# A new order of single operations within a chunk's period, and a skip term added in PSUM

## The chip, the cores and the metric

One Trainium2 chip, one core. The metric is the device time of one execution in microseconds (us). The kernel is written in Bass with the Tile framework. Its engines are TensorE (PE, with its weight loads as PEld), VectorE (DVE), ScalarE (ACT), GpSimd (POOL) and SyncE (SP, which here only issues DMAs). POOL issues DMAs too, into a queue of its own ("software dynamic" in the profile; SP's is "hardware dynamic").

## The reference

Two layers, each an S4 state-space convolution and a SwiGLU feed-forward block, on one sequence of L = 2048 positions with D = 512 channels (N = 128 states per channel, F = 1376). Cut to what matters:

```
def A(u, A_re, A_im, B, C, log_dt, Dskip):      # u is layernorm(x)
    dt = exp(log_dt)
    P  = exp(dt * (A_re + i*A_im) * l)          # l = 0 .. L-1
    K  = sum over n of (C * P * dt * B).real    # [D, L]: one filter per channel
    y  = causal convolution of u with K, along the sequence (by FFT)
    return y + u * Dskip
def B(x): return (silu(x @ w_gate) * (x @ w_up)) @ w_down
x = x + A(layernorm(x)); x = x + B(layernorm(x))   # twice, with the same weights
```

The skip term u * Dskip is a convolution with a filter that is Dskip at lag 0. So the kernel adds Dskip to the filter's value at lag 0 and has no other code for it. That one addition is "skip" below.

## The kernel before, in words

The program has two parts. The first, the **kernel stage** (until about 245 us of the span), computes the filters K and their spectra. The second takes the spectra through the convolutions and the two feed-forward blocks; a short **passage** (some 245 to 335 us), in which the weights are scaled and the first blocks are convolved, joins them. In the second part a scheduler sets the order, and the order of its instructions is the same in both kernels.

In the kernel stage the 512 channels are cut into NCH = 8 chunks of DC = 64 channels. The filter is split by lag into two factors: P over l is a product of a coarse factor (64 values, tiles `re` and `im`, in the big tile `wall`; buffer c % 2 for chunk c) and a fine one (32 values, tile `g`, two buffers). What is done for each chunk:

- `gen_turns`: phases, by integer additions on DVE (`xz` and the upper half of `im`; in the listing TENSOR_TENSOR wall<-tdk, then four ISA wall<-wall, each twice as long as the last).
- `gen_trig`, `gen_exp`: sines, cosines, exponentials on ACT, with a change of ACT's function table (ACT_TABLE_LOAD) between them.
- `gen_e`: four products on DVE that make `re` and `im` of the coarse factor.
- `gen_g`: the fine factor by doubling, n = 1, 2, 4, 8, 16. Each level is a product with the real part (L491), a product with the imaginary part into a scratch tile (L502), and an addition (L505). For n = 16 and chunks 1 to 6 the second product (L494) goes into the other, free half of the next chunk's `g` buffer, and the addition is done by a DMA with accumulation, issued by POOL (L495, g<-g, 1 MB). So this DMA stands in for a DVE addition.
- `lags`: 128 matmuls on PE (L515, L516) contract the two factors over the states: pk[32, 64] for each channel. They read all of `g`, and `re` and `im` of the chunk.
- `spread_in`: ACT copies pk out of PSUM to `ks` (L526).
- `spread`: SP writes `ks` to DRAM (`kdr`, L533) and reads it back in four DMAs, one per 32 partitions (L535), into `kt`, which has the lags on partitions. For the last two chunks `spread_pe` does it instead with 16 matmuls by pieces of the identity (L542) into `kp`, and an ACT copy to `kt` (L544).
- `skip`: adds Dskip to partition 0 of `kt` (L522). Partition 0 comes with the first of the four reads. It runs on DVE for chunks 0 to 6 and on POOL for chunk 7.
- `spectra` (for chunk 7 `first_parts` and `later_parts`): matmuls of `kt` with DFT constants (L550, L595), copies by ACT, stores to DRAM (`wo`, `spare`, `wa`). `sizes` sums |kt|.

Mixed into this are the norms of the feed-forward weights (`weights`: POOL loads pieces `st`, three buffers; ACT squares them, L353; PE sums them, L356; DVE takes the maximum, L359) and the spectra of the second input block (`second_block`).

Engines run their own instructions in order and wait for each other by semaphores. In the kernel stage no scheduler sets that order: it is written by hand, as a **plan**. A period of 28 to 31 units has one chunk in each state: `use(i)` for chunk i, `factors(i + 1)`, `prepare(i + 2)`. Each step is put into the plan at a number, `at(t + 7.1, copy)`, the plan is sorted by these numbers, and the steps are then issued one after the other. A generator is cut by `yield` into the pieces that can have a number of their own. The numbers give the order of issue only. No engine waits for one of them.

A DVE instruction that reads what an earlier DVE instruction wrote waits for a semaphore that the earlier one raises at its end.

```
            V.tensor_tensor(g[:, :, n:2 * n], g[:, :, 0:n], zr.to_broadcast([P, 2, n, DC]), OP.mult)
            if n == 16 and 0 < ch < NCH - 1:
                tmp = gs[ch + 1][:, :, 16:32]
                V.tensor_tensor(tmp, g[:, ::-1, 0:16], ...)
                G.dma_start(g[:, :, 16:32]..., tmp..., accum_op=OP.add)
```

Of the kernel before, what the change touches and what calls it, by code (L numbers as in the profile page):

```python
# [32 lines left out]
DC = 64  # L33
# [44 lines left out]
def kernel(ctx, tc, x, a_re, a_im, b_re, b_im, c_re, c_im, log_dt, d_skip,  # L78
# [114 lines left out]
    dsk, th32 = tdk[0:1, 0], tdk[:, 1]  # L193
    nc.sync.dma_start(dsk, d_skip)
# [263 lines left out]
    def gen_e(ts):  # L458


        re, im, mu = ts[:3]
        half = [[t.rearrange("p a (g h d) -> p a g h d", g=4, h=2)[:, :, :, o] for t in (re, mu)] for o in range(2)]
        V.tensor_tensor(im[:, :32], im[:, 64:32:-1], re[:, :32], OP.mult)
        yield
        V.tensor_tensor(re[:, :32], re[:, 64:32:-1], re[:, :32], OP.mult)
        yield
        V.scalar_tensor_tensor(im[:, 33:64], im[:, 31:0:-1], -1.0, mu[:, 1:], OP.mult, OP.mult)
        yield
        for r, u in half:
            V.tensor_tensor(r[:, 33:64], r[:, 31:0:-1], u[:, 1:], OP.mult)  # L470
            yield

    def gen_g(ch, ts, g):
# [11 lines left out]
        V.tensor_tensor(g[:, 1, 0], g[:, 1, 0], tmp[:, 1, 0], OP.add)  # L485
        for n in (1, 2, 4, 8, 16):
            yield
# [4 lines left out]
            if n == 16 and 0 < ch < NCH - 1:  # L492
                tmp = gs[ch + 1][:, :, 16:32]
                V.tensor_tensor(tmp, g[:, ::-1, 0:16], xz[:, 2:0:-1, lv:lv + 1].to_broadcast([P, 2, 16, DC]), OP.mult)  # L494
                G.dma_start(g[:, :, 16:32].rearrange("p i b d -> p i (b d)"), tmp.rearrange("p i b d -> p i (b d)"),  # L495
                            accum_op=OP.add)
                continue
            step = min(n, 8)
            for b0 in range(0, n, step):
                tmp = tmp8[:, :, :step]  # L500
                o = slice(n + b0, n + b0 + step)
                V.tensor_tensor(tmp, g[:, :, b0:b0 + step], zi.to_broadcast([P, 2, step, DC]), OP.mult)  # L502
                if b0 + step == n:
                    yield
                V.tensor_tensor(g[:, :, o], g[:, :, o], tmp[:, ::-1], OP.add)  # L505
        yield
# [473 lines left out]
    with tc.manual_schedule(engines={mybir.EngineType.Activation, mybir.EngineType.DVE, mybir.EngineType.PE, mybir.EngineType.Pool}):  # L980
# [30 lines left out]
        stats_x = stats(x1, 4, 1.0, then=lambda: (take(gg, 1), take(ge, 1)))  # L1011
# [4 lines left out]
        for g in (gg, gg, ge, gg, gg, gg, gg, gg, gg):  # L1016
# [12 lines left out]
        for g in (gg, ge, gg, ge, ge):  # L1029
# [14 lines left out]
        def prepare(c, t):  # L1044
# [7 lines left out]
            at(t + 0.35, steps["turns"])  # L1052
            at(t + 0.45, tr)
            at(t + 13.0, steps["turns"], 3)
            at(t + 13.2, steps["turns"], 3)
            at(t + 17.0, tr)
            at(t + 8.3, steps["exp"], 100)

        def factors(c, t):
# [7 lines left out]
            if c + 1 < NCH:  # L1067
                at(t + 8.05, lambda: tiles(c + 1))
# [3 lines left out]
            at(t + 0.3, ge)  # L1072
            for k in range(5):
                at(t + 8.2 + k, gg)
            for k in range(4):
                at(t + 22.0 + 0.6 * k, ge, 1 if k < 3 else 100)

        def use(c, t):
# [12 lines left out]
            at(t + 25.0, lambda: sizes(c, kt, box["ks"]))  # L1091
            for q0, ats in list(enumerate(((t + 17.5, t + 25.2, n + 2.1, n + 7.5),
                                      (n + 6.9, n + 14.0, n + 17.3, n + 21.0))))[:2 if c < NCH - 2 else 1]:
                sp = later(lambda q0=q0: spectra(c, kt, q0))
                if c == NCH - 2:
                    tail["sp"] = sp
                    ats = ats[:2]
                for t0 in ats:
                    at(t0, sp)

        def second_block(k, t):
            box = []
            at(t - 3.0, lambda: box.append(second(*sec[k])))
# [24 lines left out]
        for i in range(NCH - 1):  # L1128
# [6 lines left out]
            for k, t0, t1, t2, t3 in ((0, -13.0, 0.25, 13.9, 22.3), (1, 0.3, 14.5, 17.45, 22.9),  # L1135
                                      (2, 15.0, 26.5, 28.05, 36.0)):
                n = ((3, 3, 0), (3, 3, 0), (3, 3, 0), (3, 2, 0), (3, 2, 0), (3, 3, 0), (3, 3, 3))[i][k]
                if i == NCH - 2 and k == 2:
                    t0, t1, t2, t3 = 15.0, 20.0, 24.0, None
# [61 lines left out]
        spread_pe(ks, kts[1])  # L1201
        skip(c, kts[1], G)
# [109 lines left out]
```

## Time and profile before

| | |
|---|---|
| median of 3 runs | 1077.5 us (1077.13 to 1078.07) |
| the profiled execution | 1077.3 us, its span 1075.0 us |
| PE busy, of the span | 1015.1 us (94%), mean granted clock 0.985 |
| DVE busy | 966.5 us (90%) |
| ACT, POOL busy | 544.4 us (51%), 103.9 us (10%) |
| DMA | 139.74 MB, mean 130 GB/s |

The profile tells of one execution. Each row of the timeline has a start and a duration in us, the engine, the line of the code (L494), the operation and its tiles. In brackets stands how long the engine was idle before it and what ended that wait. Matmuls overlap in PE, so that PE's busy time is no measure of how near it is to its limit. For DMAs the profile has the issue (on SP or POOL) and the time from there to the landing.

### The profile page before, as it was taken

To read this page: it belongs to the slowest core of one execution; us is meant where nothing else is said; L and a number is where in the kernel's file an instruction comes from. 1 tells how busy PE (TensorE), PEld (TensorE's weight loads), DVE (VectorE), ACT (ScalarE), POOL (GpSimd) and SP (SyncE) were. 2 spreads that over 40 slices of the span, in tenths; PEclk is the share of its full clock that TensorE was granted. 3 is DMA by queue.
4 is the path that set the end of the run, shared out by engine and by line. 5 is a ranking of instruction groups with operands and counts; after the bars stand their busy time and mean duration, and the time that the engine had idled before them with its cause. 6 is when DMAs were issued, how large, how long until landed. Compare 5 with 4: busy or idle time off the path is not lost.

```text
span 1075.0 us, 22004 instructions
## 1 busy us (share of the span) xinstructions
PE 1015.1 (94%) x8918; PEld 801.8 (75%) x8918; DVE 966.5 (90%) x1405; ACT 544.4 (51%) x1093; POOL 103.9 (10%) x163
## 2 busy tenths in 40 slices
PE   1979999998789999999999999999999999999998
PEld 0868888887677787777868677786868677696774
DVE  8999999999999999999999999999999999983221
ACT  6979888853268264366652235523525442144210
POOL 1112222210000001011000001101000000000000
PEclk9989999998899999999999999999999999999999
DMA  5266777878665444323054463442444244413000
GB/s 215 100 177 180 171 165 182 188 187 270 218 207 160 122 130 151 128 94 70 16 138 140 126 212 112 124 133 100 123 120 121 86 122 139 126 36 64 1 26 20
DMA packets 120104, 139.74 MB, mean 130 GB/s; under 512 B 50609, under 2 KB 75697, under 8 KB 119234
## 3 DMA queue, kind: packets, MB, share of 16 engines
q1 hardware_dynamic: 108098, 112.83, 34.9%
q0 software_dynamic: 11904, 25.50, 10.2%
q8 instruction: 70, 1.15, 0.5%
q14 instruction: 32, 0.26, 0.1%
HBM read 91.36 MB, written 30.67 MB: 114 GB/s over the span
## 4 chain that ended last, share of the span: by engine, by line
DVE 37%; PE 27%; issue 4%; DMA 3%; ACT 3%; POOL 1%; DVEq 0%; SPq 0%; ACTq 0%; POOLq 0%
DVE t L817 5%; PE pgu L938 5%; PE pgu L935 5%; PE pgu L936 5%; DVE yk L820 5%; DVE yk L817 4%; PE py L951 3%; PE py L952 3%; PE py L953 3%; DVE sg L942 2%; DVE yl L236 2%; DVE hl L944 2%; DMA st<-in_B_w_down_dram 1%; PE pi L789 1%; PE pw L550 1%
## 5 line engine op out<-in xcount | busy, mean ns | idle before, releaser
L935 PE MATMUL pgu<-mix,wall 128*128 128x256 f16 x1280 | 299.0, 273 | 5.8 <-DVE sy L629 2.1
L936 PE MATMUL pgu<-mix,wall 128*128 128x256 f16 x1280 | 298.9, 273 | 0.0
L938 PE MATMUL pgu<-mix,wall 128*128 128x256 f16 x1280 | 195.7, 273 | 0.0
L936 PEld LDWEIGHTS <-wall 128*128 128x128 f16 x1280 | 125.2, 98 | 22.6 <-issue 7.0
L935 PEld LDWEIGHTS <-wall 128*128 128x128 f16 x1280 | 125.2, 98 | 16.4 <-issue 0.9
L938 PEld LDWEIGHTS <-wall 128*128 128x128 f16 x1280 | 125.2, 98 | 14.6
L951 PE MATMUL py<-wall,hh 128*128 128x512 f16 (+1 forms) x352 | 133.4, 379 | 0.0
L952 PE MATMUL py<-wall,hh 128*128 128x512 f16 (+1 forms) x352 | 133.4, 379 | 0.0
L953 PE MATMUL py<-wall,hl 128*128 128x512 f16 (+1 forms) x352 | 132.2, 379 | 0.0
L820 DVE TENSOR_TENSOR yk<-yk,t 128x1024 f32<-128x1024 f32 x96 | 117.5, 1224 | 0.5
L817 DVE TENSOR_TENSOR t<-uu,w 128x1024 f32<-128x1024 f32 x96 | 117.5, 1224 | 0.2
L943 ACT ACTIVATE hh<-sg 128x512 f16<-128x512 f32 x80 | 50.2, 627 | 117.4 <-DVE sg L942 117.3
L942 DVE SCALAR_TENSOR_TENSOR sg<-pgu,sc,sg 128x512 f32<-128x512 f32 x80 | 60.0, 750 | 39.2 <-ACT sg L941 39.2
L550 PE MATMUL pw<-kt,ek 128*128 128x256 f32 (+1 forms) x384 | 93.4, 381 | 0.0
L941 ACT ACTIVATE sg<-pgu,sc 128x512 f32<-128x512 f32 x80 | 54.3, 678 | 75.1 <-PE pgu L938 62.1
L550 PEld LDWEIGHTS pw<-kt,ek 128*128 128x128 f32 x384 | 75.0, 199 | 8.4
L944 DVE TENSOR_TENSOR hl<-sg,hh 128x512 f16<-128x512 f32 x80 | 55.3, 691 | 8.7 <-ACT hh L943 8.6
L953 PEld LDWEIGHTS <-hl 128*128 128x128 f16 (+1 forms) x352 | 34.3, 98 | 38.0
L952 PEld LDWEIGHTS <-hh 128*128 128x128 f16 (+1 forms) x352 | 34.4, 98 | 37.7
L951 PEld LDWEIGHTS <-hh 128*128 128x128 f16 (+1 forms) x352 | 34.4, 98 | 37.3
L515 PE MATMUL pk<-wall,g 128*32 128x64 f32 x1024 | 57.4, 288 | 4.9 <-DMA g<-g 3.7
L516 PE MATMUL pk<-wall,g 128*32 128x64 f32 x1024 | 57.8, 287 | 0.7 <-issue 0.7
(276 smaller groups left out, 1930.6 us busy)
## 6 DMA issues: line engine op xcount, KB each, us to landing
uu<-udr SPq DMA_DIRECT2D x96, 256.0 KB, 3.0
w<-wdr SPq DMA_DIRECT2D x96, 256.0 KB, 2.7
g<-g POOLq DMA_DIRECT2D x6, 1024.0 KB, 9.1
udr<-fu POOLq DMA_DIRECT2D x22, 256.0 KB, 3.2
udr<-u SPq DMA_DIRECT2D x16, 256.0 KB, 3.3
kdr<-ks SPq DMA_DIRECT2D x6, 512.0 KB, 3.1
kt<-kdr SPq DMA_DIRECT2D x24, 128.0 KB, 3.0
out_dram<-xg SPq DMA_DIRECT2D x12, 256.0 KB, 2.3
```

The source lines that it names most:

```text
L516: PE.matmul(o, lhsT=g[:, 1, :, d], rhs=im[:, 0:64, d], start=False, stop=True, tile_position=(0, 32 * grp))
L550: PE.matmul(pw[:, i], lhsT=e, rhs=kt[:, :, c + 4 * k0:4 * k1:4, :].rearrange("p g k d -> p k g d"), start=c == 0, stop=c == 3)
L817: V.tensor_tensor(t, uu.unsqueeze(2).to_broadcast([P, NQ, 2, 2, DC]), w.unsqueeze(3).to_broadcast([P, NQ, 2, 2, DC]), OP.mult)
L820: V.tensor_tensor(yk, yk, t, OP.add)
L935: PE.matmul(o, lhsT=wgu(wi, k, 0)[:, fs], rhs=nh[:, k], start=k == 0, stop=False)
L936: PE.matmul(o, lhsT=wgu(wi, k, 1)[:, fs], rhs=nh[:, k], start=False, stop=False)
L938: PE.matmul(o, lhsT=wgu(wi, k, 0)[:, fs], rhs=nlo[:, k], start=False, stop=k == 3)
L942: V.scalar_tensor_tensor(sg, pgu[:, 1], sc6[:, 4:5], sg, OP.mult, OP.mult)
L944: V.tensor_tensor(hl[:, f0:f0 + 2], sg, hh[:, f0:f0 + 2], OP.subtract)
L951: PE.matmul(py[r], lhsT=hh[:n, f, rc], rhs=wd(f, 0)[:n], start=f == 0, stop=False)
L952: PE.matmul(py[r], lhsT=hh[:n, f, rc], rhs=wd(f, 1)[:n], start=False, stop=False)
L953: PE.matmul(py[r], lhsT=hl[:n, f, rc], rhs=wd(f, 0)[:n], start=False, stop=f == FT - 1)
```

## The change

Four things are done.

1. **Single operations in the plan.** `gen_g`, `gen_e` and `gen_turns` are cut at more places, and each piece gets a number of its own. The operations on DVE (and some on ACT, PE, POOL and SP) stand in another order. The steps and their sizes stay.
2. **The skip term of the last two chunks** is added by PE: `spread_pe` has one further matmul of 128x16 into 32 partitions for each of four groups, which adds the identity's first 32 columns times `tdk`, the row of Dskip, to `kp` in PSUM. For this the other 127 rows of `tdk` are set to zero (a MEMSET on POOL at the start). The additions on DVE (chunk 6) and POOL (chunk 7) go.
3. **Squares and norms.** ACT's squares of one group of weights in each period stand directly behind `ks`, and the matmuls that sum the other group directly behind `lags`.
4. **BN_STATS and BN_AGGR** of several rows are issued in a staggered way (statistics of the next row ahead of the aggregation of this one).

```diff
+    G.memset(tdk[:, 0], 0.0)
     nc.sync.dma_start(dsk, d_skip)
...
-        for r in range(rows):
-            V.bn_stats(st[:, r], src[:, r])
-            V.bn_aggr(mv[:, r], st[:, r])
+        for r in range(rows + 1):
+            if r < rows:
+                V.bn_stats(st[:, r], src[:, r])
+            if r:
+                V.bn_aggr(mv[:, r - 1], st[:, r - 1])
...
         for n in (1, 2, 4, 8, 16):
-            yield
             V.tensor_tensor(g[:, :, n:2 * n], g[:, :, 0:n], zr.to_broadcast([P, 2, n, DC]), OP.mult)
             if n == 16 and 0 < ch < NCH - 1:
+                yield
                 tmp = gs[ch + 1][:, :, 16:32]
...
                             accum_op=OP.add)
+                yield
                 continue
...
                 V.tensor_tensor(tmp, g[:, :, b0:b0 + step], zi.to_broadcast([P, 2, step, DC]), OP.mult)
-                if b0 + step == n:
-                    yield
+                yield
                 V.tensor_tensor(g[:, :, o], g[:, :, o], tmp[:, ::-1], OP.add)
...
-    def spread_pe(ks, kt):
+    def spread_pe(ch, ks, kt):
...
                 PE.matmul(kp[32 * ga:32 * ga + 32, grp], lhsT=ident[:, 32 * grp:32 * grp + 32], rhs=ks[:, ga],
-                          start=True, stop=True, tile_position=(0, 32 * ga))
+                          start=True, stop=ga > 0, tile_position=(0, 32 * ga))
+                if ga == 0:
+                    PE.matmul(kp[:32, grp, 0], lhsT=ident[:, :32], rhs=tdk[:, 0, ch * DC + 16 * grp:ch * DC + 16 * (grp + 1)],
+                              start=False, stop=True, tile_position=(0, 0))
...
-            for k in range(4):
-                at(t + 0.2 + 2 * k, gg, 2)
+                    [0.2, 0.25, 0.339, 2.3, 2.4, 2.5, 7.316, 9.189, 13.02, 13.06, 13.131, 13.171, 13.231]:
+                at(t + d, gg)
...
-            at(t + 7.1, copy)
+            at(t + 5.104, copy)
             if c == NCH - 2:
-                at(t + 10.0, lambda: spread_pe(box["ks"], kt))
-            at(t + 13.1, lambda: skip(c, kt, V))
+                at(t + 10.0, lambda: spread_pe(c, box["ks"], kt))
+            else:
+                at(t + 13.17, lambda: skip(c, kt, V))
...
-        spread_pe(ks, kts[1])
-        skip(c, kts[1], G)
+        spread_pe(c, ks, kts[1])
```

What stands where is told by the listing of each engine's instructions. The names in it: `kt` is the filter with lags on partitions, `tdk` holds Dskip and phases, `g` the fine factor, `spare` the scratch tile, `xz` small powers, `wall` the coarse factor, `mu` squares of `re`, `cmx` maxima of weights.

DVE, the second half of a chunk's period, before (L505 of level 4 to the last of `gen_e`'s products):

```order
L505 TENSOR_TENSOR g<-g,spare 128x2x256
L491 TENSOR_TENSOR g<-g,xz 128x2x512
L502 TENSOR_TENSOR spare<-g,xz 128x1024
L505 TENSOR_TENSOR g<-g,spare 128x2x512
L491 TENSOR_TENSOR g<-g,xz 128x2x1024
L494 TENSOR_TENSOR g<-g,xz 128x2x1024
L412 TENSOR_TENSOR wall<-tdk,am 128x128
L416 ISA wall<-wall 128x256
L416 ISA wall<-wall 128x512
L522 TENSOR_TENSOR kt_425<-kt_425,tdk 1x4x16
L416 ISA wall<-wall 128x1024
L416 ISA wall<-wall 128x2048
```

The same stretch of DVE in the changed kernel (its lines are numbered 3 to 8 higher here: L512 is the addition, L495 and L510 the two products of a level, L499 the product for the DMA, L415 and L419 the phases, L529 the skip):

```order
L415 TENSOR_TENSOR wall<-tdk,am 128x128
L512 TENSOR_TENSOR g<-g,spare 128x2x256
L419 ISA wall<-wall 128x256
L495 TENSOR_TENSOR g<-g,xz 128x2x512
L510 TENSOR_TENSOR spare<-g,xz 128x1024
L419 ISA wall<-wall 128x512
L419 ISA wall<-wall 128x1024
L512 TENSOR_TENSOR g<-g,spare 128x2x512
L419 ISA wall<-wall 128x2048
L529 TENSOR_TENSOR kt_426<-kt_426,tdk 1x4x16
L495 TENSOR_TENSOR g<-g,xz 128x2x1024
L499 TENSOR_TENSOR g<-g,xz 128x2x1024
```

The phases and the skip have moved from behind the two products of the last level to ahead of them, in between the doubling's steps. Behind L499 there now come the products of `gen_e` at once.

POOL, one period before, from the DMA with accumulation on:

```order
L495 DMA g<-g 128x2x1024
L418 MEMSET wall 128x64
L347 DMA st<-in_B_w_gate_dram 128x344 x3
L553 DMA wdr<-wa 128x3x128 x2
L347 DMA st<-in_B_w_gate_dram 128x344 x2
L441 MEMSET wall 128x64
```

and in the changed kernel (L350 is the load of weights, L444 and L421 the memsets):

```order
L500 DMA g<-g 128x2x1024
L563 DMA wdr<-wa 128x3x128 x2
L350 DMA st<-in_B_w_gate_dram 128x344 x2
L444 MEMSET wall 128x64
L350 DMA st<-in_B_w_gate_dram 128x344 x3
L421 MEMSET wall 128x64
```

Three loads of weights no longer stand right behind the DMA with accumulation, but ahead of the next period's.

PE, the filter of chunk 7 turned by `spread_pe`, before:

```order
L542 MATMUL kp<-ks,ident 32x256 x16
```

and in the changed kernel:

```order
L549 MATMUL kp<-ks,ident 32x256
L552 MATMUL kp<-tdk,ident 32x16
L549 MATMUL kp<-ks,ident 32x256 x4
L552 MATMUL kp<-tdk,ident 32x16
L549 MATMUL kp<-ks,ident 32x256 x4
L552 MATMUL kp<-tdk,ident 32x16
L549 MATMUL kp<-ks,ident 32x256 x4
L552 MATMUL kp<-tdk,ident 32x16
L549 MATMUL kp<-ks,ident 32x256 x3
```

Four small matmuls were put in, and POOL's addition (L522 TENSOR_TENSOR, 1x4x16) is gone.

More of the change, by code (lines that the diff above doesn't have):

```diff
@@ L1010 @@
         take(tn, 7)
-        stats_x = stats(x1, 4, 1.0, then=lambda: (take(gg, 1), take(ge, 1)))
+        stats_x = stats(x1, 4, 1.0, then=lambda: (take(gg, 1), take(ge, 1), take(gg, 1)))
         tr = gen_trig(ts[1])
@@ L1015 @@
         take(tr, 1)
-        for g in (gg, gg, ge, gg, gg, gg, gg, gg, gg):
+        for g in (gg, gg, ge, gg, gg, ge, gg, gg, gg):
             take(g, 1)
@@ L1028 @@
                 nc.sync.dma_start(ndr[h, cp], x1[:, 2 * cp:2 * cp + 2, h * HD:(h + 1) * HD])
-        for g in (gg, ge, gg, ge, ge):
+        for g in (gg, gg, gg, ge, gg, gg, ge, ge):
             take(g, 1)
@@ L1051, in prepare @@
             tr = later(lambda: gen_trig(ts[c]))
[L1052 to L1057, printed above, removed]
+            for d in [0.35, 13.0, 13.04, 13.08, 13.12, 13.16, 13.161]:
+                at(t + d, steps["turns"])
+            for d in [0.45, 17.0]:
+                at(t + d, tr)
+            for d, n in [(8.726, 100)]:
+                at(t + d, steps["exp"], n)
         def factors(c, t):
```

41 lines of the change are left out of this document (21 added, 20 removed).

## The prediction

> **What bounds the kernel now.** First the stages: the answer that cuts the span at the ends of the kernel stage (235 us), of the passage (335 us) and of DVE's dense work (930 us).
>
> ```profile
> core 0: us, PE busy (x) PEld busy (x) DVE busy (x) ACT busy (x) POOL busy (x), PEclk, DMA share, GB/s
> 62.00:235.00 173.00, 160.98 (x2085) 138.72 (x2084) 170.36 (x203) 144.82 (x322) 41.33 (x62) 0.96 0.73 175
> 235.00:335.00 100.00, 82.91 (x722) 73.51 (x721) 94.48 (x144) 48.35 (x98) 8.97 (x8) 0.91 0.73 222
> 335.00:930.00 595.00, 591.04 (x4667) 453.37 (x4667) 586.48 (x873) 264.59 (x508) 44.20 (x64) 1.00 0.40 120
> ```
>
> DVE is busy 170.36 of the 173 us in the kernel stage, and the list of waits has none of DVE's between 60 and 235 us. DVE's own stream sets the period. Behind it everything follows DVE (94.5 and 98.6% busy) or PE, in an order that the change leaves alone, so I take a shift at the stage's end through to the end of the program.
>
> Next, what DVE loses though it never waits: its timeline in the last level of the doubling.
>
> ```profile
> 118.64 1.22 DVE L491 TENSOR_TENSOR g<-g,xz 128x1024 f32<-128x1024 f32 x1
> 119.78 1.22 DVE L502 TENSOR_TENSOR spare<-g,xz 128x1024 f32<-128x1024 f32 x1
> 121.04 1.23 DVE L505 TENSOR_TENSOR g<-g,spare 128x1024 f32<-128x1024 f32 x1
> 122.30 2.29 DVE L491 TENSOR_TENSOR g<-g,xz 128x2048 f32<-128x2048 f32 x1
> 124.51 2.28 DVE L494 TENSOR_TENSOR g<-g,xz 128x2048 f32<-128x2048 f32 x1
> 126.71 0.28 DVE L412 TENSOR_TENSOR wall<-tdk,am 128x128 int32<-128x128 int32 x1
> ...
> 127.70 0.20 DVE L522 TENSOR_TENSOR kt<-kt,tdk 1x64 f32<-1x64 f32 x1
> 127.83 1.94 DVE L416 CUSTOM_DVE_ANT_0 wall<-wall 128x1024 uint16<-128x1024 uint16 x2
> ```
>
> L502 reads nothing that L491 wrote, and starts 1.14 us after it: 0.08 before its end. L505 reads what L502 wrote, and starts 1.26 after it, 0.04 behind its end; so does L491 behind L505. A neighbour that depends costs 0.12 us.
>
> Last, the way from one period to the next that is not on DVE. The product L494 ends at time E, here 96.83 + 2.28 = 99.11.
>
> ```profile
> 96.83 2.28 DVE L494 TENSOR_TENSOR g<-g,xz 128x2048 f32<-128x2048 f32 x1
> 99.41 1.26 POOL L495 DMA_DIRECT2D g<-g  x1 [9.74 <-DVE wall L412]
> 108.04 1.19 DVE L470 TENSOR_TENSOR wall<-wall,mu 128x992 f32<-128x992 f32 x1
> 108.62 0.46 PE L515 MATMUL pk<-wall,g 128*32 128x64 f32 x8 [0.54 <-DMA g<-g]
> 116.70 1.02 ACT L526 ACTIVATE ks<-pk 128x1024 f32<-128x1024 f32 x1 [0.15 <-PE pk L516]
> 117.75 0.34 SPq L533 DMA_DIRECT2D kdr<-ks  x1
> 121.15 1.74 SPq L535 DMA_DIRECT2D kt<-kdr  x4
> ...
> L494 DVE TENSOR_TENSOR g<-g,xz x6: 2283/2284/2285, 69.7 to 206.6; 128x2048 f32<-128x2048 f32 x6
> ```
>
> POOL issues the DMA with accumulation at E + 0.30, `lags` starts on PE at E + 9.51, when that DMA has landed, ACT copies at E + 17.6, and `kt` is read back from E + 22.0 on. The skip waits for it at E + 28.6 (127.70) with time to spare, and L491 and L494 stand ahead of the skip. So this way is no loop: DVE issues the next DMA without having waited for this one's filter. Six L494 in 206.6 - 69.7 us make a period of 27.38.
>
> **The change, part by part.**
>
> *Neighbours that depend.* I counted them in the two listings: 186 before, 136 after. 50 x 0.12 = 6.0 us is the most that the single operations can give on DVE: 11 pairs ahead of the first L494 (1.3 us), 32 in the five intervals between the six products (60 before, 28 after: 0.8 us each), 7 behind the last (0.8). The BN statistics are among them. In the rules for kernel authors the Trainium skill (VectorE: DVE Perf Modes, "The DRAIN you can't avoid" and "Rules for kernel authors") speaks against this part: the next operation cannot issue before the pipe is empty, a semaphore after each costs nothing extra, and what counts is the number of operations. By that rule this term is 0 instead of 6.0. The rows above do not agree: 1.14 against 1.26 for operations of one size.
>
> *The loop.* In the new order the skip of a chunk stands ahead of the two products of the last level, and the phases too, which overwrite what `lags` of the same period reads. So a chain closes: product, DMA, `lags`, copy, `kdr`, `kt`, skip, product. All its links are rows of before. Landing times:
>
> ```profile
> g<-g POOLq DMA_DIRECT2D x6, 1024.0 KB, 9.1
> DMA to landing us min/median/max: 8.9/9.1/9.2
> ...
> kdr<-ks SPq DMA_DIRECT2D x6, 512.0 KB, 3.1
> DMA to landing us min/median/max: 2.6/3.1/3.5
> ...
> L535 SPq DMA_DIRECT2D kt<-kdr x24: 318/424/555, 66.2 to 203.8; - x24
> DMA to landing us min/median/max: 2.6/3.0/3.2
> ...
> 82.09 0.45 PE L515 MATMUL pk<-wall,g 128*32 128x64 f32 x8
> 89.80 1.01 ACT L526 ACTIVATE ks<-pk 128x1024 f32<-128x1024 f32 x1
> ```
>
> (The three landing rows belong to g, `kdr` and `kt`.) From E: 9.51 to `lags`. From there to ACT's copy 8.08 in the chain above and 7.71 here. In the first, the DVE product L470 ended only at 109.23, inside `lags`. In the new order it is done 2 us ahead, so I take 7.75, near the lower. 1.05 to the write of `kdr` (116.70 to 117.75), 3.1 for its landing, 0.05 to the first read. The skip needs partition 0 alone, which the first of four reads brings: 2.6, the shortest landing. A hop of 0.1, 0.13 for the skip (127.70 to 127.83), 4.49 for the two products (122.30 to 126.79). Sum: 9.51 + 7.75 + 1.05 + 3.1 + 0.05 + 2.6 + 0.1 + 0.13 + 4.49 = 28.8 us for each turn. DVE's own stream would need 27.38 - 0.8 = 26.6. DVE thus waits about 2 us in each period, first for `lags` ahead of the phases, then for `kt`.
>
> Bounds of a turn: with the shortest links (8.9, 7.6, 2.6, 2.6) 28.0, with the longest (9.2, 8.08, 3.5, 3.2) 30.2. Even if `kt` came at once the wait for `lags` would hold it at 28: 9.5 to their start, 7.3 for the matmuls (7.71 less the hop to ACT), then from L415 to the skip 2.9 for the phases (126.71 to 129.7, without the skip), 3.7 for three steps of doubling (118.64 to 122.30), 0.6 for one of half their size, less 0.5 for the pairs, then 4.6 for skip and products.
>
> The price: five turns between six products, 5 x (28.8 - 27.38) = +7.1 us. The 1.3 ahead of the first product is kept, as is the 0.8 behind the last. The five times 0.8 inside are swallowed.
>
> *The skip in PSUM.* Chunk 6: 0.13 us of DVE goes. Chunk 7, in the passage:
>
> ```profile
> 258.16 1.85 POOL L522 TENSOR_TENSOR kt<-kt,tdk 1x64 f32<-1x64 f32 x1 [15.52 <-ACT kt L544]
> 260.06 0.43 PE L595 MATMUL pw<-kt,ef 128*128 128x64 f32 x2 [3.08 <-POOL kt L522]
> 266.49 1.23 DVE L817 TENSOR_TENSOR yk<-mix,w0r 128x1024 f32<-128x1024 f32 x1 [1.20 <-ACT w0r L596]
> ```
>
> POOL's 1.85 us go, PE starts L595 that much sooner (less the four new matmuls, some 0.06 us each by the rows of 8 in 0.45), and the 1.20 that DVE waits for its result is covered: -1.2, at worst 0 if PE is held there by something else.
>
> *The rest, at nothing.*
>
> ```profile
> 1.62 0.09 POOL L153 MEMSET hpi<- 128x1 f32 x1
> 10.67 0.30 SPq L194 DMA_DIRECT2D tdk<-in_A_Dskip_dram  x1
> ```
>
> The new MEMSET stands on POOL right behind that of `hpi`, and SP's DMA into the row is issued 9 us later: neither queue waits. The four matmuls in chunk 6 lie under PE's wait for `ks`. The squares behind `ks` delay ACT's exponentials by 1.2 us and save it the same later. The moved loads leave POOL's queue free ahead of the DMA, which was issued 0.30 after E and will be again.
>
> *Sum.* +7.1 - 1.3 - 0.8 - 0.1 - 1.2 = +3.7 us on the profiled execution's 1077.3, which is 0.2 under the median of the runs. So 1081.
>
> **The rivals.**
>
> *DVE goes free (faster).* The loop stays under 26.6, DVE never waits, and all pairs count: -6.0 - 0.1 - 1.2 = -7.3, 1070 us. For this the turn must lose 2.2 us, and only the DMA with accumulation has them: it would have to land in 6.9 us instead of 9.1. The loads of weights that now follow it directly share its queue and the 16 DMA engines, and they go away from there. If the engines served all evenly, the 516 KB of three loads would stretch its 1024 KB by half. Against it:
>
> ```profile
> 102.00:104.00 2.00, 2.00 (x11) 1.77 (x10) 2.00 (x2) 1.88 (x1) 2.00 (x3) 1.00 1.07 180
> ...
> st<-in_B_w_gate_dram POOLq DMA_DIRECT2D x16, 172.0 KB, 9.0
> st<-in_B_w_up_dram POOLq DMA_DIRECT2D x16, 172.0 KB, 4.6
> ```
>
> The engines are full (1.07) from 102 on at 180 GB/s, so 1 MB takes 5.8 us and the rest is start and end; and loads issued behind it land at 9.0, as if in turn after it, where elsewhere they take 4.6. For its length the Trainium skill (DMA: Bandwidth & Descriptors, "Anatomy of one DMA — SWDGE (gpsimd) path") has 2 us and the bytes at 436 GB/s, an estimate of 4.4 us for 1 MB, by which the turn would be 24.1 and this rival right. The landing row has 9.1 in its place.
>
> *A shorter turn.* The DMA gains a half of that (1 us), the turn is 27.4 to 27.9: 1074 to 1077.
>
> *ACT becomes the bound (slower).*
>
> ```profile
> 102.12 1.91 ACT L428 ACTIVATE wall<-wall 128x2048 f32<-128x2048 int32 x1 [1.89 <-DVE wall L416]
> 107.16 2.01 ACT L430 ACTIVATE wall<-wall,hpi 128x2048 f32<-128x2048 f32 x1
> 110.21 0.29 DVE L481 TENSOR_TENSOR g<-w,wall 128x128 f32<-128x128 f32 x1
> ```
>
> ACT reaches the sines with 1.89 us to spare, and DVE needs the last of them 1.04 after its end. In the new order DVE comes to that step about 3 us sooner behind the product (the phases are no longer between), and on ACT the squares stand right behind the copy of `lags`' result. If these then wait for weights that land after 9.0 us, not 4.6, ACT falls 4 us behind, and the first step of `gen_g` waits for it in some periods: two or three times 4 us, 1090.
>
> **How the numbers follow.** The loop at 28.0 to 30.2 a turn gives 1077 to 1088; I hold it at 0.70, with 0.15 of that within 0.2% of before (2.2 us, about what a measurement of this kernel can tell from no change). DVE free 0.13; the shorter turn 0.09, half of it faster, half the same; ACT 0.08. So faster 0.17, same 0.20, slower 0.63. The time is the loop's, 1081; the range 1076 to 1088 takes in its bounds and the upper half of the shorter turn, and leaves out DVE free and most of ACT.
>
> **What would show it.** Right: in the list of waits DVE has a new row on L415 (for PE pk) or L529 (for a DMA kt), 1 to 3 us each, five or six times; the L499 stand 28 to 29.5 us apart; PE waits 9 us for the DMA with accumulation where it now waits half a microsecond; a pair of L510 and L512 that still stands together costs 0.12 more than one that does not; the POOL row of the skip is gone, and so is DVE's 1.20 on `w0r`. Wrong: L499 under 27 us apart, or a landing of g under 8 us; a wait of L485 for ACT would speak for the third rival.

## The result: 1092.05 us, slower by 1.3%, and the profile after

| | before | changed |
|---|---|---|
| median of the runs | 1077.5 us (1077.13 to 1078.07) | 1092.05 us (1089.1 to 1093.39) |
| ratio | | 1.0131 (95% interval 1.0108 to 1.0154) |
| the profiled execution, its span | 1077.3, 1075.0 us | 1089.1, 1087.3 us |
| second product of the last level, six times | 27.38 us apart | 29.25 us apart |

Forecast were 1081 us and 1076 to 1088. The direction was right, the size was not: +3.7 us were forecast on the profiled execution, and +11.8 measured, outside the range. (The other executions of the changed kernel lie 2 to 4 us above the profiled one; why was not tried.)

First the stages of the changed kernel, cut at the same times as before: busy times of the engines, PE's granted clock, DMA share.

```profile
core 0: us, PE busy (x) PEld busy (x) DVE busy (x) ACT busy (x) POOL busy (x), PEclk, DMA share, GB/s
62.00:235.00 173.00, 148.91 (x1929) 130.80 (x1932) 158.26 (x194) 142.98 (x319) 41.19 (x61) 0.91 0.71 165
...
335.00:930.00 595.00, 589.21 (x4655) 452.31 (x4654) 586.02 (x879) 270.56 (x520) 46.87 (x64) 1.00 0.41 121
```

In the kernel stage DVE has fallen from 170.36 to 158.26 us of 173. It is no longer what sets the period. In the dense part behind, it is as busy as before (586.02 against 586.48). What it waits for in the stage is told by its list of waits (total us, times, longest), here of the first 400 us. The last line is from PE's list:

```profile
DVE wall L415 <- PE pk L523: 6.0, 4, 3.3
DVE kt L529 <- DMA kt<-kdr: 4.7, 5, 1.4
DVE wo L588 <- ACT w0r L584: 3.5, 1, 3.5
...
DVE kt L529 <- ACT wall L446: 1.1, 1, 1.1
...
PE pk L522 <- DMA g<-g: 15.8, 5, 3.5
```

The two new rows are the phases (L415) behind `lags` and the skip (L529) behind `kt`. One period in DVE's timeline shows both:

```profile
119.93 0.29 DVE L415 TENSOR_TENSOR wall<-tdk,am 128x128 int32<-128x128 int32 x1 [0.84 <-PE pk L523]
...
127.11 0.21 DVE L529 TENSOR_TENSOR kt<-kt,tdk 1x64 f32<-1x64 f32 x1 [0.47 <-DMA kt<-kdr]
127.25 2.27 DVE L495 TENSOR_TENSOR g<-g,xz 128x2048 f32<-128x2048 f32 x1
129.45 2.27 DVE L499 TENSOR_TENSOR g<-g,xz 128x2048 f32<-128x2048 f32 x1
...
L499 DVE TENSOR_TENSOR g<-g,xz x6: 2271/2272/2273, 72.5 to 218.7; 128x2048 f32<-128x2048 f32 x6
```

L415 waits until `lags` is done; 11.8 us later L499 ends, of which 0.47 is the wait for `kt`. The product's end starts the next DMA with accumulation, and the chain is closed. The last row gives the period: the first and the last start, 72.45 and 218.69 before rounding, lie five turns apart, 29.25 each.

The landing times of the three transfers in that chain (KB each, median us from issue to landing), and what POOL issues beside `kdr`:

```profile
g<-g POOLq DMA_DIRECT2D x6, 1024.0 KB, 8.7
...
kdr<-ks SPq DMA_DIRECT2D x6, 512.0 KB, 4.1
...
kt<-kdr SPq DMA_DIRECT2D x24, 128.0 KB, 3.7
...
91.63 0.32 SPq L540 DMA_DIRECT2D kdr<-ks  x1
...
92.42 1.59 POOL L350 DMA_DIRECT2D st<-in_B_w_gate_dram  x3 [1.65 <-ACT sq L356]
...
94.77 1.76 SPq L542 DMA_DIRECT2D kt<-kdr  x4
```

The DMA with accumulation is 0.4 us shorter than before (9.1), `kdr` 1.0 longer (3.1), `kt` 0.7 longer (3.0). Three loads of weights are issued between `kdr` and `kt`: POOL waits with them for ACT's squares (L356), which now stand directly behind `ks`.

**Where the 12.3 us of the span came from**, by the ends of the first and the last of the six products and of L588 of chunk 6 (in before L578):

| stretch | before | changed | difference | forecast |
|---|---|---|---|---|
| start to the end of the first product | 72.02 | 74.73 | +2.7 | -1.3 |
| first to last product, five turns | 136.88 | 146.24 | +9.4 | +7.1 |
| last product to the end of L588 | 39.6 | 39.5 | -0.1 | -0.9 (0.8 of neighbours, 0.1 of chunk 6's skip) |
| from there to the end of the span | 826.5 | 826.9 | +0.4 | -1.2 |

### The profile page after: what moved, and what is told of

Its sections match the earlier page's. It is cut to its first block, busy times and chain, and to the rows that moved or that the text cites. A ratio compares the mean times of both kernels' runs of the same rounds, so it can differ in the third digit from the quotient of the medians.

```text
span 1087.3 us, 22050 instructions
## 1 busy us (share of the span) xinstructions
PE 1011.9 (93%) x8934; PEld 800.5 (74%) x8934; DVE 963.0 (89%) x1404; ACT 544.5 (50%) x1093; POOL 103.7 (10%) x163
## 4 chain that ended last, share of the span: by engine, by line
PE 34%; DVE 30%; issue 3%; ACT 2%; DMA 2%; POOL 1%; SPq 0%; DVEq 0%; ACTq 0%; POOLq 0%
PE pgu L945 6%; PE pgu L946 6%; PE pgu L948 6%; DVE t L827 4%; DVE yk L830 4%; DVE yk L827 4%; PE py L962 3%; PE py L963 3%; PE py L961 3%; PE pi L799 2%; DVE sg L952 2%; DVE yl L239 2%; DVE hl L954 2%; DVE z L239 1%; DVE fbt L239 1%
## 5 line engine op out<-in xcount | busy, mean ns | idle before, releaser
L945 PEld LDWEIGHTS <-wall 128*128 128x128 f16 x1280 | 125.2, 98 | 17.4 <-issue 1.9
L522 PE MATMUL pk<-wall,g 128*32 128x64 f32 x1024 | 57.6, 290 | 20.9 <-DMA g<-g 15.8
L522 PEld LDWEIGHTS pk<-wall,g 128*32 128x32 f32 x1024 | 51.6, 140 | 24.0 <-issue 24.0
```

Of the source, the lines that this page charges most:

```text
L522: PE.matmul(o, lhsT=g[:, 0, :, d], rhs=re[:, 0:64, d], start=True, stop=False, tile_position=(0, 32 * grp))
L945: PE.matmul(o, lhsT=wgu(wi, k, 0)[:, fs], rhs=nh[:, k], start=k == 0, stop=False)
```

## The experiments

Each run was timed against the kernel before on its own chip (medians there 1076.25, 1076.35 and 1076.28 us in three groups). A ratio is of the run to that kernel before. The table gives what the readings rest on: the distance of the six products of the last level, the ends of the first and the last of them, the end of L588, and what is left of the span behind it ("rest").

| run | median, ratio (95% interval) | apart | first, last | L588 ends | rest |
|---|---|---|---|---|---|
| before | 1077.5 | 27.38 | 72.0, 208.9 | 248.5 | 826.5 |
| changed | 1092.05, 1.0131 (1.0108 to 1.0154) | 29.25 | 74.7, 221.0 | 260.4 | 826.9 |
| e1 before, skip ahead | 1093.62, 1.0156 (1.0140 to 1.0173) | 29.95 | 74.9, 224.7 | 265.0 | 827.1 |
| e2 changed, skip elsewhere | 1082.83, 1.0062 (1.0047 to 1.0077) | 28.33 | 73.4, 215.0 | 254.5 | 828.8 |
| e3 changed, loads back | 1088.71, 1.0118 (1.0103 to 1.0133) | 29.32 | 74.4, 221.0 | 260.6 | 825.8 |
| e4 before, skip in PSUM | 1075.72, 0.9992 (0.9982 to 1.0001) | 27.37 | 72.1, 208.9 | 248.7 | 825.6 |
| e5 changed, both gates open | 1073.06, 0.9971 (0.9959 to 0.9983) | 26.76 | 71.7, 205.5 | 245.0 | 825.8 |
| e6 changed, `kt` gate alone | 1086.07, 1.0092 (1.0077 to 1.0108) | 29.98 | 75.0, 224.9 | 265.3 | 817.8 |
| e7 e5, squares back | 1070.48, 0.9947 (0.9927 to 0.9967) | 26.70 | 71.7, 205.2 | 247.0 | 821.3 |
| e8 interleaved | 1067.33, 0.9919 (0.9905 to 0.9933) | 26.81 | 72.1, 206.2 | 246.9 | 817.6 |
| e9 in one piece | 1069.13, 0.9937 (0.9924 to 0.9949) | 27.43 | 71.3, 208.4 | 248.9 | 819.0 |
| e10 before, phases ahead | 1077.11, 1.0009 (0.9999 to 1.0020) | 27.69 | 74.9, 213.4 | 253.8 | 820.1 |

**e1: one instruction of the kernel before moved.**

```diff
-            at(t + 13.1, lambda: skip(c, kt, V))
+            at(t + (10.12 if c < 5 else 13.1), lambda: skip(c, kt, V))
```

> The kernel before, with one instruction of each of chunks 0 to 4 moved: DVE's skip stands six places earlier, ahead of the last L505 and the products L491 and L494 instead of behind three of the phases. Nothing else moves, the second part's order included. Theory 1 (the loop: product, accumulating DMA, lags, ks, kdr, kt, skip, product): a turn is 9.4 to lags + 7.8 to ks + 1.05 + 5.7 for kdr and kt (mean of the rows of before) + 0.1 + 5.9 from the skip to the end of L494 = 29.9 us, so L494 stand 29.9 apart instead of 27.4, DVE waits for DMA kt at the skip 2 to 3.5 us in each period, and the time is about 1077.5 + 4 x 2.5 (chunks 1 to 4 close a turn each) + 3 at chunk 0 = 1090. Theory 2 (the time of the changed kernel comes from its squares, loads or exponentials on ACT and POOL, not from the skip's place): none of these moved, so within 1 us of 1077.5.

Measured: 1093.62 us, +17.4. The waits of DVE, and one period:

```profile
DVE kt L522 <- DMA kt<-kdr: 12.5, 4, 4.6
DVE kt L522 <- ACT wall L455: 3.0, 1, 3.0
...
100.82 0.21 DVE L522 TENSOR_TENSOR kt<-kt,tdk 1x64 f32<-1x64 f32 x1 [4.62 <-DMA kt<-kdr]
100.96 1.21 DVE L505 TENSOR_TENSOR g<-g,spare 128x1024 f32<-128x1024 f32 x1
...
104.41 2.28 DVE L494 TENSOR_TENSOR g<-g,xz 128x2048 f32<-128x2048 f32 x1
```

An operation of 0.13 us, put six places earlier, costs more than the whole change. Four closed turns took 31.8, 29.7, 29.7 and 31.1 us, 30.6 in the mean (29.9 expected); the fifth, with the skip in its old place, took 27.5. The one wait of 3.0 stands under ACT in the list, but it is the skip of chunk 0 that waits, and nothing else about it changed. So the loop exists, and it needs no other part of the change. The cost was 4 us above the 13 of the expectation: 2.9 from the longer turns, 0.8 and 0.6 from the two stretches behind the last product.

**e2: the skip in its new place, but without `kt`.**

```diff
-                at(t + 13.17, lambda: skip(c, kt, V))
+                at(t + 13.17, lambda: V.tensor_tensor(dk, dk, dk, OP.max))   # dk = dsk[:, c * DC:(c + 1) * DC]
```

> The changed kernel, with DVE's skip of chunks 0 to 5 replaced by an operation of the same size on the row of Dskip itself: it stands in the same place and waits for no kt. The skip term is left out of these six chunks. Order of all engines and of the second part as in the changed kernel. Theory 1 (the loop through kt): the gate through kt (turn 29.25 us) is gone, and the next one is L415 behind lags: 9.2 + 7.5 + 11.2 from L415 to the end of L499 = 27.9. Five turns give 6.7 us, and the wait at chunk 0 another 1.1: 1092 - 7.8 = 1084; L499 27.6 to 28.3 apart, and L415 waits in five or six periods. Theory 2 (the price is on ACT or in the lower clock of PE): 1090 or more. Theory 3 (DVE alone would set the period once kt is out): 26.6 apart, 1078.

The kernel leaves out the skip term of chunks 0 to 5. Measured: 1082.83 us, 28.33 apart. Two of DVE's waits in the stage:

```profile
DVE wall L415 <- PE pk L523: 6.6, 4, 3.7
DVE wo L588 <- ACT w0r L584: 3.5, 1, 3.5
```

Without `kt` the turn is 28.3 instead of 29.25, and not the 26.6 that DVE alone would need: the second gate, the phases behind `lags`, then holds DVE by itself. The first product ends 1.4 us sooner (73.4), which gives the wait of 1.1 at chunk 0 to `kt`, too. Against the kernel before on its own chip this run is 6.6 us slower, where the changed kernel is 14.6.

**e3: the loads back behind the DMA with accumulation.**

```diff
-            for k, t0, t1, t2, t3 in ((0, -18.289, 0.25, 2.189, 9.83), ...
+            for k, t0, t1, t2, t3 in ((0, -13.0, 0.25, 2.189, 9.83), ...
```

> The changed kernel, with the three loads of weights (st) that POOL issued at the time of kdr and kt put back behind the DMA with accumulation, where they stood before. DVE, PE, ACT and SP have the same order as in the changed kernel. Theory 1 (these loads share the DMA engines with kdr and kt and lengthen them from 5.7 to 6.7 us): kdr and kt together back at 5.6 to 5.9, L499 28.2 to 28.5 apart instead of 29.25, the wait at chunk 0's skip gone or under 0.3: 1092 - 5 x 0.9 - 1 = 1086.5. Theory 2 (kdr and kt are longer for another reason, or the loads cost as much behind the accumulating DMA, by lengthening it): L499 29 apart or more, 1091 to 1094.

Measured: 1088.71 us; its interval overlaps the changed kernel's. Landings and waits:

```profile
g<-g POOLq DMA_DIRECT2D x6, 1024.0 KB, 9.1
...
kdr<-ks SPq DMA_DIRECT2D x6, 512.0 KB, 3.1
kt<-kdr SPq DMA_DIRECT2D x24, 128.0 KB, 3.0
...
DVE wall L415 <- PE pk L523: 10.0, 4, 4.3
...
DVE kt L529 <- DMA kt<-kdr: 0.6, 2, 0.4
```

The first half of theory 1 is shown: the loads made `kdr` and `kt` longer, and away from them both are back at 3.1 and 3.0. The second half is not: the turn stays at 29.3. The wait only went from the skip (4.7 to 0.6) to L415 (6.0 to 10.0). The way from the copy to the skip is 0.8 us shorter in the mean of the five turns. But the DMA with accumulation, with the loads directly behind it, takes 9.1 again, and `lags` starts 0.5 later behind the product; and `lags` itself was 0.2 to 0.7 us longer in four chunks (the stalls of the last section), 0.4 in the mean. This is theory 2's other branch, though the time lies between the two theories. The wait at the skip of chunk 0 stayed, too (1.0, in the list under "issue"). What the loads no longer took at `kt`, the gate through `lags` took.

**e4: only the skip in PSUM, on the kernel before.** The diff is the `spread_pe` part and the MEMSET of the change.

> The kernel before, with the skip of chunks 6 and 7 added in PSUM by PE and the MEMSET of tdk, and nothing else of the change; the second part's order is that of before. Theory 1 (the 1.2 us that DVE waits for w0r behind POOL's addition are a cost of their own): the POOL row and DVE's wait are gone, 1077.5 - 1.3 = 1076.2. Theory 2 (another wait, for PE or ACT, stands right behind it, or the second part takes it back): within 0.4 of 1077.5.

Measured: 1075.72 against 1076.25 us, a ratio of 0.9992 (0.9982 to 1.0001): theory 1's 1.3 us lies inside the interval, and so does nearly nothing. In the trace the last addition is gone, and the DVE row that waited 1.20 before has no wait:

```profile
265.62 1.23 DVE L821 TENSOR_TENSOR yk<-mix,w0r 128x1024 f32<-128x1024 f32 x1
```

It starts 0.87 us sooner than its fellow in before (266.49), although chunk 6's product ahead of it ended 0.2 later, so the local price was near 1.1. In the time it is lost among the differences of the second part (the rest was 825.6 to 828.8 in all seven kernels with its old order, with the skip in PSUM or without).

**e5: both gates open.** Two rows of numbers, for the phases and for the skip:

```diff
-            for d in [0.35, 13.0, 13.04, 13.08, 13.12, 13.16, 13.161]:
+            for d in [0.35, 13.1, 13.15, 13.2, 13.235, 13.24, 13.241]:
                 at(t + d, steps["turns"])
...
-                at(t + 13.17, lambda: skip(c, kt, V))
+                at(t + 13.238, lambda: skip(c, kt, V))
```

> The changed kernel with two things moved in DVE's order, and nothing else (the other engines and the second part keep the changed kernel's order): the phases stand later, L415 behind L510 of the last full level and its steps between L512, L495, L499, with the two largest behind L499; and the skip stands behind L499. Dependent neighbours: 141 (186 before, 136 in the changed kernel), 7 in each interval between the products. Theory 1 (the two gates, kt ahead of the skip and lags ahead of L415, make all the loss): from L415 to the end of L499 only 6.4 us, so the turn through lags is 9.2 + 7.4 + 6.5 = 23.1 and no gate any more; DVE alone sets the period, 27.38 - 5 x 0.12 = 26.75. First product at 72.0 (six pairs fewer, but three phases of 0.8 us ahead of it), last one at 205.8 against 208.9 before; the way from there to L588 stays 39.5, then the 1.1 of POOL's skip: about -4 in all, 1072 against 1076.2 for before. Theory 2 (squares, loads or the lower clock of PE make a part of it): L499 over 28 apart and above 1080. Theory 3 (the loop is open but the pairs are worth nothing): 27.3 apart, 1075 to 1076.

Measured: 1073.06 us. No wait of DVE on L415 or L529 is left, and the period:

```profile
118.89 0.28 DVE L415 TENSOR_TENSOR wall<-tdk,am 128x128 int32<-128x128 int32 x1
...
122.97 2.28 DVE L499 TENSOR_TENSOR g<-g,xz 128x2048 f32<-128x2048 f32 x1
125.17 0.68 DVE L419 CUSTOM_DVE_ANT_0 wall<-wall 128x1024 uint16<-128x1024 uint16 x1
125.77 0.20 DVE L529 TENSOR_TENSOR kt<-kt,tdk 1x64 f32<-1x64 f32 x1
...
L499 DVE TENSOR_TENSOR g<-g,xz x6: 2284/2284/2287, 69.4 to 203.2; 128x2048 f32<-128x2048 f32 x6
```

(203.2 - 69.4) / 5 = 26.76, where 26.75 was expected; first and last product within 0.3 us of it. Everything else of the change is still there (squares, loads, exponentials, PE's matmuls), so the two gates are the whole loss in the loop. With them open the change is 3.3 us (0.3%) faster than the kernel before.

**e6: the gate through `kt` alone.** As e5, with the skip left at 13.17.

> As the run with both gates open, but the skip stands ahead of the last two products (one instruction differs in the kernel stage): only the gate through kt is closed, the one through lags open. The second part comes in another order here, so the distance of the products counts and the time only roughly. Theory 1 (either gate is enough): 9.2 to lags, 7.5 to ks, 1.05, 6.7 for kdr and kt, 0.1, then skip, L495, one L419, L499 = 5.0: 29.5 us from L499 to L499, DVE waits 2 to 4 us for DMA kt at the skip and nowhere for PE pk at L415; about 1090. Theory 2 (only the phases behind lags count, kt comes early enough by itself): 27.3 apart or less, under 1080.

```profile
DVE kt L529 <- DMA kt<-kdr: 15.4, 5, 4.6
DVE kt L529 <- ACT wall L458: 3.4, 1, 3.4
```

29.98 apart, no wait at L415, 1086.07 us. With e2 (28.33), the changed kernel (29.25) and e5 (26.76) that completes the square: either gate alone is enough, the one through `kt` is the longer, and the two don't add up. That this run lies above the changed kernel fits two links of its chain: from the skip to the end of L499 it takes 4.95 us against 4.61, since one step of the phases stands between the products here, and from the write of `kdr` to the first read it takes 0.5 more.

**e7: the squares back.** As e5, with the row of numbers for `weights` as in the kernel before.

> The run with both gates open, and the squares, norms, maxima and loads of the weights back in the places of the kernel before (part 3 of the change undone). The second part comes in another order, so the distance of the products counts and the time only within 2 us. Theory 1 (squares and norms lie beside DVE's work and are worth nothing): L499 26.6 to 26.9 apart as with both gates open, no wait of DVE for ACT in the stage, within 2 us of that run. Theory 2 (squares directly behind ks keep ACT late and cost, by L485 waiting for the sines or by the loads beside kdr): at least 0.3 us less per period than with both gates open. Theory 3 (their new place is a gain): at least 0.3 more per period.

26.70 apart against 26.76: theory 1. Squares and norms have no part in the period while the gates are open. The landings say once more what the loads do: with them back in their old place `kdr` and `kt` take 2.7 and 2.9 us, in e5 3.7 and 3.6. (Its time, 1070.48 us, is 2.6 below e5's and so outside the expected 2 us, although L588 ends 2 us later; the gain is in the rest, 821.3 against 825.8, where the order is another.)

**e8 and e9: two orders of the phases with the same second part.** e8 sets the phases at 13.03, 13.09, 13.15, 13.2, 13.24, between the last operations; e9 at 14.0 to 14.4, in one piece behind them; both have the skip behind L499.

> The changed kernel with the phases between the last two levels' operations, but near enough to the products that lags should not hold them, and the skip behind L499: 130 dependent neighbours, 5 or 6 in each interval. The second part comes in the order that it had in the run with the gate through kt alone, where it took 817.8 us from the end of chunk 6's L588 to the end of the span, against 825.6 to 828.8 in the seven runs with the order of the kernel before. From L415 to the end of L499 it is 9.3 us, so the gate through lags is 9.2 + 7.4 + 9.4 = 26.0, just under DVE's own 27.38 - 6.3 x 0.12 = 26.6. Theory 1: L499 26.6 apart (27.9 once, where lags takes 9.3), the last at 205.4 to 206.7, L588 ended at 245 to 246, and 817.8 + 245 + 2.3 = 1065 us, faster than both kernels. Theory 2 (the second part's 817.8 belonged to that run's late stage and not to its order): 1072 to 1074. Theory 3 (a turn of 26.0 is too near, lags holds the phases in most periods): L415 waits for PE pk in four or five periods, L499 27.5 or more apart, 1069 or more.

> As the interleaved run beside it, with the same second part, but the five operations of the phases stand in one piece behind the products and the skip, as in the kernel before: 172 dependent neighbours, 12 or 13 in each interval, 7 more than in the interleaved one. No gate is closed. Theory 1 (a neighbour that depends costs 0.12 us): L499 27.45 apart, 0.8 more than interleaved, the last at about 208.4, L588 ended at 247 to 248, time 2 to 3 us above the interleaved run. Theory 2 (only the number of operations counts): the same distance in both, the same time within 1 us.

The products of e8, then of e9, and e8's one wait at L415:

```profile
L499 DVE TENSOR_TENSOR g<-g,xz x6: 2284/2285/2286, 69.8 to 203.9; 128x2048 f32<-128x2048 f32 x6
...
DVE wall L415 <- PE pk L523: 0.5, 1, 0.5
```
```profile
L499 DVE TENSOR_TENSOR g<-g,xz x6: 2283/2284/2287, 69.0 to 206.1; 128x2048 f32<-128x2048 f32 x6
```

26.8 against 27.4: seven neighbours fewer in a period save 0.62 us, 0.09 each (0.12 was booked; without the wait of 0.5 it would be 0.10). That is theory 1 of e9. Of the 2.3 us that e8 is ahead of e9 at the last product, 2.0 are left at L588, where both wait for ACT, and 1.8 in the time (2 to 3 were expected). The gate at 26.0 held in one period of five, for 0.5 us: e8 is about as early as the phases can stand. It is the fastest version here, 1067.33 us, 2 us above what its theory 1 gave; L588 ended at 246.9 and not by 246. But most of the 9.0 us that it is below before is not the stage's: before's L588 ends 1.6 us later than e8's, and the rest is 817.6 against 826.5. e9 has before's period and is 7.2 us faster than before by its rest alone.

**e10: the phases ahead, on the kernel before.**

```diff
-            at(t + 13.0, steps["turns"], 3)
-            at(t + 13.2, steps["turns"], 3)
+            at(t + 10.1, steps["turns"], 3)
+            at(t + 10.15, steps["turns"], 3)
```

> The kernel before, with the five operations of the phases moved as one piece ahead of the last L505, L491 and L494 (the skip stays behind L494). The second part comes in another order, so the distance of the products counts and the time only roughly. Theory 1 (the order of a piece costs only where a turn gets longer than DVE's own period): from L412 to the end of L494 8.7 us, turn 9.5 + 7.6 + 8.7 = 25.8, under 27.4: L494 27.2 to 27.6 apart, no wait of DVE in the stage. Theory 2 (phases ahead of the products cost in any place): a wait at L412 for PE pk in most periods and L494 over 28 apart.

```profile
DVE wall L412 <- PE pk L516: 0.2, 1, 0.2
...
L494 DVE TENSOR_TENSOR g<-g,xz x6: 2284/2285/2286, 72.7 to 211.1; 128x2048 f32<-128x2048 f32 x6
```

27.7 apart, one wait of 0.2, the time as before: theory 1 on the waits, though the distance is 0.1 over its range. What it shows besides: the first product ends at 74.9 instead of 72.0. The phases of 2.9 us now stand ahead of the first product as well, and from the last product to L588 it takes 40.4, not 2.9 less than 39.6. What goes ahead of a chain that ends late is not got back behind it.

## Why the prediction was right or wrong

**What was missing.** On the span 3.7 us were forecast and 12.3 measured. Of the 8.6 between, 4.0 lie ahead of the end of the first product, 2.3 in the five turns, 0.8 in the tail behind the last product and 1.6 in the rest.

**Neighbours that depend.** Right in kind. The Trainium skill's rule (VectorE: DVE Perf Modes, "The DRAIN you can't avoid" and "Rules for kernel authors"), by which the number of operations alone counts, would give e8 and e9 one period; they differ by 0.62 us. The first of these sections also says that a next operation that is not held starts earlier; the rows of L502 and L505 in the prediction agree (1.14 against 1.26 us from start to start). The term was 0.12 each, measured 0.09 between e8 and e9 and 0.12 between e4 and e5 (27.37 to 26.76, five neighbours fewer in each period, though these two differ in more).

**The first product: the step that failed most.** "11 pairs ahead of the first L494 (1.3 us)" and "The 1.3 ahead of the first product is kept". It ended 2.7 later, a mistake of 4.0 us. The sum counted the pairs there and not the phases that move to that place. Within the five intervals one set of phases goes out and one comes in. But there are six products and five intervals: ahead of the first product a set comes in and none goes out.

```profile
62.31 0.28 DVE L415 TENSOR_TENSOR wall<-tdk,am 128x128 int32<-128x128 int32 x1
...
67.78 1.22 DVE L419 CUSTOM_DVE_ANT_0 wall<-wall 128x2048 uint16<-128x2048 uint16 x1
70.11 0.21 DVE L529 TENSOR_TENSOR kt<-kt,tdk 1x64 f32<-1x64 f32 x1 [1.11 <-ACT wall L446]
...
72.45 2.27 DVE L499 TENSOR_TENSOR g<-g,xz 128x2048 f32<-128x2048 f32 x1
```

That is 2.7 us for the five operations of the phases (from the start of each to that of its successor), 0.1 of skip and a wait of 1.1; the sum less the 2.7 that were measured leaves 1.2 for the pairs, near the 1.3 booked. The wait is a part of the loop that I had not followed into chunk 0, which has a `kt` though no turn yet. e10 shows the phases alone (the first product 2.9 later), e2 the wait.

**The loop.** Right in its mechanism and both gates (e1, e2, e5, e6), and 29.25 lies within its bounds of 28.0 and 30.2. The sum of 28.8 was 0.5 too small, five times: +9.4 instead of +7.1. Link by link, in the mean of the five turns of the profiled execution:

| link | booked | measured |
|---|---|---|
| end of the product to the start of `lags` | 9.51 | 9.02 |
| from there to ACT's copy | 7.75 | 7.86 |
| to the write of `kdr` | 1.05 | 1.05 |
| to the first read into `kt` | 3.15 | 3.46 |
| to the skip | 2.70 | 3.25 |
| skip and two products | 4.62 | 4.61 |

The links that were too short are `kdr` and `kt`, 0.9 together; the DMA with accumulation gave 0.5 back, so that the bounds held in part because errors offset each other. I had put the moved loads "at nothing" with an eye on the DMA ahead of which they no longer stand, and did not ask where they would go: to the new place of the squares that free their buffers, between `kdr` and `kt`. I had put the shorter-turn rival on their leaving; the effect was there (8.7 instead of 9.1), and e3 shows that it is worth about what it costs. The second link hides a stall: it took 9.34 us for chunk 4, where PE stood still inside `lags` (last section), and 7.38 to 7.57 for the others. In a closed chain that stall goes straight into the turn: 30.8 us for chunk 4, 28.9 in the mean of the other four.

**The tail.** "as is the 0.8 behind the last": not kept. From the last product a chain of its own runs through the DMA, `lags`, the matmuls that stand behind it on PE (in the changed kernel PE works from 230.3 to 258.5 with no wait in its timeline), ACT's copies and L588. These rows are of before and of after:

```profile
206.61 2.29 DVE L494 TENSOR_TENSOR g<-g,xz 128x2048 f32<-128x2048 f32 x1
...
247.55 0.96 DVE L578 TENSOR_TENSOR wo<-pw,wo 128x768 f32<-128x768 f32 x1 [0.24 <-ACT w0r L574]
```
```profile
218.69 2.27 DVE L499 TENSOR_TENSOR g<-g,xz 128x2048 f32<-128x2048 f32 x1
...
259.49 0.96 DVE L588 TENSOR_TENSOR wo<-pw,wo 128x768 f32<-128x768 f32 x1 [3.46 <-ACT w0r L584]
```

39.6 us and 39.5. In before DVE waited 0.24 at its end, the sign of a chain that is just as long as DVE's work; DVE's gain there became a wait of 3.46. I had read DVE's waits for `w0r` at L817 only, and not at L578.

**The skip in PSUM.** The wait of 1.2 us is gone from that place (e4). Whether it shows in the time is not settled: e4's interval holds both, and in the changed kernel the rest was 826.9, no shorter than before.

**The rivals.** DVE free was wrong for this order. With both gates open it is right in kind: DVE alone sets the period, and the kernel is 3.3 us faster than before (e5; that rival had 7.3). For the length of its DMA the estimate from the Trainium skill (DMA: Bandwidth & Descriptors, "Anatomy of one DMA — SWDGE (gpsimd) path") was 4.4 us; the row has 8.7. ACT as the bound came to nothing: DVE's list has no wait of L489 (the old L485), and e7 moved nothing in the period. Of the signs named ahead, "PE waits 9 us for the DMA with accumulation" was wrong: it waits 15.8 us in five waits, 3.2 each (a sixth, of 3.7, stands under ACT), since PE has the spectra of the chunk before to do meanwhile.

**Still open.** Why the second part is 4 to 11 us shorter in another order. By DVE's instructions in the traces, before, changed and e1 to e5 have one order there, with a rest of 825.6 to 828.8; e6, e8, e9 and e10 have another, 817.6 to 820.1; and e7 has a third, 821.3. That the order does it and not the stage is shown by e6, e8 and e9, whose stages end up to 18 us apart with one second part; by which of its waits was not looked into.

## What to carry to other kernels

Before an operation on a busy engine is put ahead of another, however small it is, follow what the other one starts (a DMA, another engine's matmuls) until the chain either ends or comes back to the moved operation: if it comes back, its length is a period, and it must be below what the engine needs by itself. Where two such gates are nearly of one length, opening one brings the period down only to the other: e2, with one open, still lost 6.6 of the 14.6 us; e5, with both open, gained 3.3. In a loop with n products and n - 1 intervals a moved block is paid once at the head, and given back at the tail only where DVE, and not a chain, ends last there.

## What the runs showed of the hardware that was not expected

- *PE stalls at one place of `lags`, and goes on behind a load of instructions.* Its 256 matmuls take 7.3 us, but for chunk 4 they took 8.4 in before, 9.3 in the changed kernel, 9.5 in e2 and 9.7 in e3, most of it in one gap (0.8 to 2.0 us from one start to the next) behind the 153rd or 154th matmul, 4.3 or 4.4 us from the start. The trace has it as "issue" (the engine waited for nothing that the profile shows):

```profile
174.58 0.45 PE L523 MATMUL pk<-wall,g 128*32 128x64 f32 x3
176.33 0.34 PE L522 MATMUL pk<-wall,g 128*32 128x64 f32 x4 [1.30 <-issue]
```

  In the prediction I gave the 8.08 us of another chunk to a late DVE product; that chunk has such a gap, too (0.45 us behind the 202nd matmul), and so has the same chunk of e3 (0.36). The traces also list the DMA packets of the instruction queue (q8, 16 KB each). For chunk 4 such a packet starts 2.7 to 4.1 us after `lags` in the nine kernels whose gap is 0.5 us or more, and PE goes on 2.2 to 2.4 us after the packet's start in all nine. In e5, e6 and e9 it starts 1.7 us after `lags`, and there is no such gap. So PE seems to stand still for want of instructions. No run moved the packet by itself, and why it comes later in some kernels is open.
- *Where the record has a lower granted clock, `lags` took no longer.* Two rows of before:

```profile
136.31:143.60 7.29, 7.29 (x257) 7.10 (x257) 7.15 (x14) 7.26 (x14) 1.18 (x2) 0.77 0.66 125
...
190.84:198.10 7.26, 7.26 (x257) 7.07 (x257) 7.16 (x14) 7.23 (x14) 1.39 (x3) 1.00 0.81 165
```

  The same matmuls took 7.29 us at 0.77 and 7.26 at 1.00 (its row ends 0.03 ahead of the last matmul), and 7.29 at 0.66 in e3. Their starts are 27.5 ns apart where the clock record has 0.5 as where it has 1.00. In several runs `lags` took 7.41, at 0.77 (changed) as at 1.00 (e5). In the changed kernel the clock was 0.72 to 0.85 in six chunks, in before 0.77 to 1.00; for `lags` that was no part of the loss. Whether PE ran at the lower clock there at all, these rows can't tell.
